# Delta-rule attention and two feed-forward layers on one core: a queue order from step-by-step rules, replaced by a list schedule over a recorded graph

## The chip, the cores and the metric

One core of a Trainium2 chip runs the program. The metric is device time in microseconds (us) of one execution; three runs of the kernel before are shown, and the profile is of one execution. TensorE (PE) multiplies, with weight loads beside it (PEld); VectorE (DVE), ScalarE (ACT) and GpSimd (POOL) do elementwise work; SyncE (SP) issues the DMAs. Each engine takes its own queue strictly in order, so the order in which the program writes instructions is the order in which they wait.

## The reference, cut to what matters

```
# q, k, v: (4, 8, 768, 48)   beta: (4, 8, 768)
k_n = k / (norm(k) + 1e-6)
for t in range(768):                       # per batch and head, state is 48 x 48
    y[t]  = q[t] @ state
    v_old = state^T k_n[t]
    state += beta[t] * outer(k_n[t], v[t] - v_old)
x = y as (3072 tokens, 384)
x = leaky(x @ w1_in) @ w1_out              # leaky(h) = max(0.01 h, h), d_ff 2048
out = (h - tanh(h)) @ w2_out               # h = x @ w2_in
```

The recurrence runs over the sequence; the two feed-forward layers (FFN) need all heads of a token and nothing of later tokens. The kernel works in pairs of 16-bit numbers (a high and a low part of each value, three products for each matrix product).

## The kernel before

**Work.** The sequence is cut into 12 blocks of 64 positions, n = 0 to 11; two of them make a unit, u = 0 to 5. The attention of a block is done in chunked form: `keys` normalizes and splits the keys, `grams` transposes them (matmuls with `ident2`) and forms the products of keys with keys (matmuls `KTp`, `KTp`) into the tile `Gd`; `inverses` (once per unit) solves a triangular system of 32 columns, row by row, into the tile `X`: 30 steps of two small elementwise instructions, `Gd<-X` and `X<-X,Gd`, each on what the one before left; `merges` (matmuls `X`, `AT` and then `XF`, `PM`) puts the halves together; `states`, `products` and `outputs` carry the state on and give the block's tokens, 256 of them over four batches. `to_xa` scales and splits them into a room `x`. That is the first FFN's input.

**FFN.** `layer(n, i)` does block n through layer i, in the order of units: first layer for both blocks of the unit, then second layer for both. A layer has 8 parts; a part is `h_part` (18 matmuls of 256 columns, then the activation, then a split into `g`, whose low half is a subtraction of two tiles in SBUF) and, three parts later, `o_part` (18 matmuls of 256 columns, or in the second layer 12 of 384). `to_xb` scales the first layer's result for the second.

**Weights.** The four weight matrices arrive as 64-bit floats. `w_f32` turns a chunk into 32-bit floats with three passes on DVE; `convert` adds up squares on ACT; then a scale is known and `splits` makes the 16-bit halves (one pass on ACT, one on DVE, one DMA). The raw chunks wait in parts of other weight tiles (`wo`, `wi1`), in two `x` rooms and in the tile `stage`.

**What sets the order.** Everything is issued while Python runs, by rules that look at modelled clocks (`Plan`, with its `cost` and `issue`). The FFN loop is in front: `h_part` calls `Side.step` after every second or third matmul, and `Side` lets a waiting attention or weight generator go on where its inputs are ready by the model and where `idle` says that ACT and DVE are not too far ahead of PE. Thirty numbers each in `START` and `STEADY` (delays per generator, leads, biases) shape it. Elementwise work with two possible engines is placed when it comes up: `tt` takes POOL or DVE for the low half of `g`, the key splits and the masks of `P`; `cp` takes ACT or DVE for copies. The inverse of unit 0 runs on DVE, the others on POOL (`rows` in the tables). Tiles that turn over (`x` 4 rooms, `sx` 4, `g` 4) come from pools by tag. All instructions carry line 160, the one line of `Plan.issue`.

Of the kernel before, what the change touches and what calls it, by code (L numbers as in the profile page):

```python
# [1 line left out]

# [15 lines left out]
KS = 64.0  # L18
POW2 = 0x7F800000
START = {'cp': 1.0, 'lag': 4.0, 'look_pool': 5, 'look_inv': 0, 'lead_k': 1, 'lead_p': 8.2, 'd_v': 1, 'd_xa': 0, 'd_xb': 1, 'k_m': 1, 'd_s0': 4.0, 'd_s1': 2.5, 'd_s2': -1, 'd_s3': 2.7, 'bias_i': 3.5, 'bias': 1.5, 'rep': 3, 'every': 3, 'd_k0': 3, 'd_o': 0.5, 'd_s': 0.0, 'd_p': 1.5, 'd_m': 0, 'd_i': 3, 'd_g0': -2, 'd_q': 4.4, 'd_g': 0.2, 'd_k': 1, 'd_w': 1.5, 'rows': 2}  # L20
STEADY = {'cp': 5.5, 'lag': 3.7, 'look_pool': 5, 'look_inv': 2.5, 'lead_k': 1, 'lead_p': 6.8, 'd_v': 1, 'd_xa': -1.3, 'd_xb': 1, 'k_m': 1, 'd_s0': 1.0, 'd_s1': -0.5, 'd_s2': -1, 'd_s3': 0.5, 'bias_i': 3, 'bias': 4, 'rep': 6, 'every': 2, 'd_k0': 3, 'd_o': 0.5, 'd_s': 0.0, 'd_p': 0, 'd_m': 1.5, 'd_i': 0, 'd_g0': -0.7, 'd_q': 3.4, 'd_g': 0.7, 'd_k': 0, 'd_w': 0, 'rows': 32}


class Plan:
# [3 lines left out]

    GAP = 0.15
    TICK, WARM = 10.24 / 3, 3060  # L30

    def __init__(self, nc):
        self.t = dict(pe=0.0, act=0.0, dve=0.0, pool=0.0, sp=0.0)
        self.dma = 0.0
        self.columns = {}
        self.mem = {}
        self.ring = {}
        self.filler = None
        self.eng = dict(pe=nc.tensor, act=nc.scalar, dve=nc.vector, pool=nc.gpsimd, sp=nc.sync)

    def tile(self, pool, shape, dtype, tag, name, bufs):
        t = pool.tile(shape, dtype, tag=tag, name=name, bufs=bufs)
        old = self.ring.setdefault((id(pool), tag), [])
        free = self.last(old[-bufs]) if len(old) >= bufs else 0.0
        old.append(t.tensor.name)
        self.mem[t.tensor.name] = [(0, 128, 0, 1 << 30, free, True, "")]
        return t

    def free(self, pool, tag, bufs):
        old = self.ring.get((id(pool), tag), [])  # L50
        return self.last(old[-bufs]) if len(old) >= bufs else 0.0

    def last(self, name):
        return max([e[4] for e in self.mem[name]], default=0.0)

    @staticmethod
    def region(ap):
        step, n = ap.ap[0]
        size = SIZE[ap.dtype]
        lo = ap.offset % step  # L60
        hi = lo + 1 + sum(s * (c - 1) for s, c in ap.ap[1:])
        return ap.offset // step, ap.offset // step + n, lo * size, hi * size

    def after(self, ap, write, eng=""):
        es = self.mem.get(ap.tensor.name)
        if not es:
            return 0.0
        p0, p1, lo, hi = self.region(ap)
        psum = ap.space == bass.MemoryType.PSUM
        t = 0.0  # L70
        for q0, q1, l, h, te, w, e in es:
            if (w or write or psum) and not (eng == "pe" and e == "pe"):
                if psum or (p0 < q1 and q0 < p1 and lo < h and l < hi):
                    t = max(t, te + self.GAP)
        return t

    def at(self, *aps):
        return max(self.after(a, False) for a in aps)

    def note(self, ap, t, write, eng):  # L80
        p0, p1, lo, hi = self.region(ap)
        es = self.mem.setdefault(ap.tensor.name, [])
        es[:] = [e for e in es if not ((write or not e[5] and e[6] == eng) and p0 <= e[0] and e[1] <= p1
                                       and lo <= e[2] and e[3] <= hi)]
        es.append((p0, p1, lo, hi, t, write, eng))

    def warm(self, t):

        return self.columns.get(int(t / self.TICK) - 1, 0) >= self.WARM

    def cost(self, eng, op, aps, accum=False):
        n = 1
        for a in aps:
            m = 1
            for d in a.shape[1:]:
                m *= d
            n = max(n, m)
        if eng == "pe":
            n = 1
            for d in aps[-1].shape[1:]:  # L100
                n *= d
            rows = 0.52 if aps[1].shape[0] <= 64 else 1.0
            return rows * n / (2400.0 if self.warm(self.t["pe"]) else 1200.0) + 0.001
        if eng == "act":
            return 0.1 + n * 0.0008 + (0.15 if accum else 0.0)
        if eng == "pool":
            return 0.1 + n * (0.0009 if op == "memset" else 0.002)
        fast = all(SIZE[a.dtype] == 2 for a in aps)
        sbuf = all(a.space != bass.MemoryType.PSUM for a in aps)
        r = 960.0  # L110
        if op == "memset":
            r = 1920.0
        elif op == "transpose":
            r = 480.0
        elif op in ("tensor_copy", "tensor_scalar") and sbuf:
            r = 3840.0 if fast and op == "tensor_copy" else 1920.0
        return 0.065 + n / r

    def ready(self, eng, reads, writes):
        t = 0.0  # L120
        for a in reads:
            t = max(t, self.after(a, False, eng))
        for a in writes:
            t = max(t, self.after(a, True, eng))
        return t

    def finish(self, eng, op, reads, writes):
        return max(self.t[eng], self.ready(eng, reads, writes)) + self.cost(eng, op, writes + reads)

    def issue(self, eng, op, args, kw):  # L130
        writes = [kw[n] for n in ("out", "accum_out") if n in kw]
        rest = list(args)
        if "out" not in kw:
            writes.append(rest.pop(0))
        isap = lambda a: hasattr(a, "tensor")
        reads = [a for a in rest + [v for n, v in kw.items() if n not in ("out", "accum_out")] if isap(a)]
        if eng == "sp":
            s = self.t["sp"]
            for a in writes:
                s = max(s, self.after(a, True))  # L140
            for a in reads:
                s = max(s, self.after(a, False))
            self.t["sp"] = s + 0.05
            self.dma = max(self.dma, s) + kw["out"].free_nbytes() * 128 / 300e3
            t = self.dma + 2.0
        else:
            if self.filler and eng == "dve":
                self.filler(self.ready(eng, reads, writes))
            s = self.t[eng] = max(self.t[eng], self.ready(eng, reads, writes))
            t = self.t[eng] = s + self.cost(eng, op, writes + reads, "accum_out" in kw)  # L150
            if eng == "pe":
                n = int(t / self.TICK)
                self.columns[n] = self.columns.get(n, 0) + writes[0].free_nbytes() // 4 * reads[0].shape[0] // 128
        for a in writes:
            if a.tensor.name in self.mem or a.space != bass.MemoryType.DRAM:
                self.note(a, t, True, eng)
        for a in reads:
            if a.space != bass.MemoryType.DRAM:
                self.note(a, t, False, eng)
        return getattr(self.eng[eng], op)(*args, **kw)  # L160


class Part:


    def __init__(self, aps, banks):
        self.aps, self.banks = aps, banks


class Engine:  # L170
    def __init__(self, plan, name):
        self.plan, self.name = plan, name

    def __getattr__(self, op):
        return lambda *args, **kw: self.plan.issue(self.name, op, args, kw)


class Room:


    def __init__(self, plan, pool, bufs):
        self.plan, self.pool, self.bufs = plan, pool, bufs

    def tile(self, shape, dtype, name, tag=None, bufs=None):
        return self.plan.tile(self.pool, shape, dtype, tag or name, name, bufs or self.bufs)

    def free(self, tag, bufs=None):
        return self.plan.free(self.pool, tag, bufs or self.bufs)


@with_exitstack
def kernel(
    ctx: ExitStack,
    tc: tile.TileContext,
    q: bass.AP,
    k: bass.AP,
    v: bass.AP,
    beta: bass.AP,
# [3 lines left out]
    w2_out: bass.AP,  # L202
    out: bass.AP,
):
    plan = Plan(tc.nc)
    pe, act, dve, pool, sp = (Engine(plan, n) for n in ("pe", "act", "dve", "pool", "sp"))
    NU, D = k.shape[0], k.shape[4]
    NM = k.shape[3]
# [133 lines left out]
    def at(*aps):  # L342
        return plan.at(*aps)
# [894 lines left out]
```

## Time and profile before

| what | us |
|---|---|
| three runs: lowest, median, highest | 1198.43, 1198.58, 1199.84 |
| span of the profiled execution, first to last instruction | 1199.5 |
| PE busy | 1005.0 (84%), 16216 matmuls |
| DVE busy | 738.1 (62%) |
| ACT busy | 592.5 (49%) |
| POOL busy | 419.2 (35%) |
| chain that ended last, by engine | PE 48%, DVE 25%, POOL 12%, ACT 8% |
| mean granted clock of TensorE | 0.974 of full |

The profiled execution's own time is not listed apart from its span; the span lies 0.9 us over the median of the three runs and inside their spread. An engine's busy share is a mean over stages that differ: the first eighth of the span prepares weights and the first block, the middle mixes attention with FFN, and the last quarter is nearly FFN alone. A group's line shows busy time, the mean length of one instruction in ns, and the idle time before it with what ended it.

### The profile page before, as it was taken

What the parts mean: (1) busy time and instruction counts of PE and PEld (TensorE: products, weight loads), DVE (VectorE), ACT (ScalarE), POOL (GpSimd) and SP (SyncE); (2) the same over time, 40 slices, a digit from 0 to 9 for tenths busy, and PEclk for the clock granted to TensorE, in tenths of its full rate; (3) what the DMA queues carried; (4) which work ended last, traced back from release to release, by engine and by line L of the source; (5) the groups of instructions that cost most, each with busy time, mean ns of one, the idle gap of its engine ahead of it and who ended that gap; (6) DMA issues with size and microseconds to landing.
All of it is one profiled execution on the core that took longest, in us unless ns stands there. A gap on an engine that the chain in (4) does not pass through costs nothing.

```text
span 1199.5 us, 36733 instructions
## 1 busy us (share of the span) xinstructions
PE 1005.0 (84%) x16216; PEld 823.4 (69%) x16216; DVE 738.1 (62%) x1600; ACT 592.5 (49%) x1311; POOL 419.2 (35%) x520
## 2 busy tenths in 40 slices
PE   0200887499798998987999989999999999999998
PEld 0200866387476886765788867788877888778875
DVE  7998789877567665678658666456673154420242
ACT  3533566755355764464555734535543354333332
POOL 4201033259312793168414861386110230012100
PEclk9999999799898999989999999999999999999999
DMA  9440325311101200011100100001000000000001
GB/s 361 156 134 23 109 70 181 118 61 34 28 21 29 60 1 16 3 47 27 35 25 25 32 15 17 15 2 34 25 11 14 15 11 2 14 14 1 1 1 27
DMA packets 30559, 54.45 MB, mean 45 GB/s; under 512 B 4800, under 2 KB 16064, under 8 KB 30400
## 3 DMA queue, kind: packets, MB, share of 16 engines
q1 hardware_dynamic: 30400, 52.11, 13.8%
q8 instruction: 126, 2.06, 0.7%
q14 instruction: 33, 0.27, 0.1%
HBM read 41.09 MB, written 4.72 MB: 38 GB/s over the span
## 4 chain that ended last, share of the span: by engine, by line
PE 48%; DVE 25%; POOL 12%; ACT 8%; issue 5%; DMA 2%; SPq 0%; POOLq 0%; DVEq 0%; ACTq 0%
PE o L160 19%; PE h_ps L160 18%; PE a_ps L160 11%; POOL X L160 6%; POOL Gd L160 4%; DVE wi L160 4%; DVE wo L160 2%; DVE x L160 2%; DVE X L160 2%; DVE g L160 2%; ACT g L160 2%; DVE Gd L160 2%; DVE sx L160 1%; DVE Ub L160 1%; DVE Sb L160 1%
## 5 line engine op out<-in xcount | busy, mean ns | idle before, releaser
L160 PE MATMUL h_ps<-x,wi 128*128 128x256 f16 x3456 | 433.6, 279 | 24.7 <-DVE sx L160 13.3
L160 PEld LDWEIGHTS <-wi 128*128 128x128 f16 x3456 | 338.9, 100 | 91.0 <-issue 35.4
L160 PE MATMUL o<-wo,g 128*128 128x384 f16 x1152 | 210.8, 331 | 7.3 <-ACT osb L160 4.8
L160 PE MATMUL o<-g,wo 128*128 128x256 f16 x1728 | 210.4, 274 | 1.3 <-DVE osb L160 1.3
L160 POOL TENSOR_TENSOR g<-sx,g 128x512 f16<-128x512 f32 x74 | 88.9, 1201 | 320.1 <-ACT g L160 313.7
L160 PEld LDWEIGHTS <-wo 128*128 128x128 f16 x1728 | 166.4, 98 | 25.1 <-issue 3.7
L160 ACT ACTIVATE g<-sx 128x512 f16<-128x512 f32 x192 | 121.0, 630 | 122.1 <-DVE sx L160 119.0
L160 PEld LDWEIGHTS <-g 128*128 128x128 f16 x1152 | 111.9, 99 | 74.6 <-issue 13.6
L160 DVE SCALAR_TENSOR_TENSOR sx<-sx,kap,h_ps 128x512 f32<-128x512 f32 x96 | 71.0, 740 | 96.9 <-ACT sx L160 96.4
L160 DVE SCALAR_TENSOR_TENSOR g<-sx,g 128x512 f16<-128x512 f32 x96 | 76.6, 798 | 67.1 <-ACT g L160 67.1
L160 ACT ACTIVATE sx<-h_ps 128x512 f32<-128x512 f32 x96 | 56.6, 590 | 102.9 <-PE h_ps L160 100.2
L160 ACT ACTIVATE sx<-h_ps,kap 128x512 f32<-128x512 f32 x96 | 65.4, 682 | 81.1 <-PE h_ps L160 72.3
L160 POOL TENSOR_TENSOR X<-X,Gd 128x30 f32<-128x30 f32 (+9 forms) x150 | 97.2, 648 | 11.8
L160 PEld LDWEIGHTS <-KTp 64*64 64x64 f16 x3360 | 63.4, 115 | 53.0 <-issue 49.7
L160 POOL TENSOR_TENSOR P<-P,maskp 128x1024 f16<-128x1024 f16 x24 | 56.3, 2348 | 120.9 <-DVE P L160 115.7
L160 POOL TENSOR_TENSOR Gd<-X 128x30 f32<-128x30 f32 (+9 forms) x150 | 89.0, 593 | 26.4 <-DVE X L160 14.9
L160 PE MATMUL a_ps<-ab,ones 128*128 128x1 bf16 x124 | 11.3, 166 | 101.1 <-DVE ab L160 100.6
L160 PEld LDWEIGHTS <-KN 64*64 64x64 f16 x1824 | 37.2, 119 | 38.5 <-issue 30.7
L160 DVE COPY Ub<-R 64x768 f16<-64x768 f16 x46 | 24.4, 530 | 39.7 <-PE a_ps L160 39.2
L160 POOL MEMSET XF<- 32x512 f32 x12 | 6.2, 519 | 112.9 <-PE a_ps L160 109.9
L160 PEld LDWEIGHTS <-ones 128*128 128x128 bf16 x124 | 7.8, 100 | 52.5 <-issue 38.3
L160 PE MATMUL a_ps<-Q,Sb 128*128 128x64 f16 x528 | 32.8, 194 | 10.8 <-DVE Sb L160 10.8
(163 smaller groups left out, 1451.2 us busy)
## 6 DMA issues: line engine op xcount, KB each, us to landing
wo<-in_w_in_dram SPq DMA_DIRECT2D x32, 384.0 KB, 6.2
qf<-in_q_dram SPq DMA_DIRECT2D x24, 256.0 KB, 3.0
wi<-in_w_out_dram SPq DMA_DIRECT2D x14, 384.0 KB, 7.8
kf<-in_k_dram SPq DMA_DIRECT2D x12, 384.0 KB, 3.4
vf<-in_v_dram SPq DMA_DIRECT2D x12, 384.0 KB, 3.2
out_dram<-osb SPq DMA_DIRECT2D x48, 96.0 KB, 2.2
wi<-wh SPq DMA_DIRECT2D x16, 192.0 KB, 2.7
wo<-wh SPq DMA_DIRECT2D x16, 192.0 KB, 2.5
```

The lines of the kernel that those rows point to most:

```text
L160: return getattr(self.eng[eng], op)(*args, **kw)
```

## The change

The kernel body now records instead of issuing. `Graph.put` and `Graph.matmul` make nodes (a run of matmuls into one bank is one node), `depend` draws the edges from overlapping reads and writes, `tails` computes for each node the longest path to the end, and `schedule` walks through time: of the nodes that are ready on an engine it takes the one with the longest path. `issue` then writes out that order. `START`, `STEADY`, `Plan`, `Side` and all generators go. Where two engines are allowed for a node (`either`), the schedule picks one when the node comes up.

```diff
+    def tails(self, share=1.2, stretch=1.0, extra=1.0):
+        for n in reversed(self.nodes):
+            t = tail[n.idx]
+            for m in n.succs:
+                t = max(t, tail[m.idx] + self.LAT[m.main])
...
+            a, b = heap[e]
+            if b and lock <= t + 1e-9 and (not a or b[0] < a[0]):
+                p, i, alt = heappop(b)
+            elif a:
+                p, i, alt = heappop(a)
...
-    NA, NX, NSX = 4, 4, 4
...
+    x_r = ring("x", 6, KT * N, order=False)
+    x_r.most["a"] = 5
+    s_r = ring("sx", 4, 512, short=True)
+    g_r = ring("g", LAG + 1, 512)
...
-    stage = wts.tile([128, 2 * DM * 2], F32, name="stage")
...
+    def inv_eng(u):
+        return "dve" if u == 0 else "pool"
...
+    def p_engs(n):
+        return ("dve",) if n < 4 else ("pool",)
...
+    def k_engs(n):
+        return ("dve",)
...
         if i == 0:
             copy(g[:, 0], sx)
-            tt(g[:, 1], sx, g[:, 0], ALU.subtract, bias())
+            tt(g[:, 1], sx, g[:, 0], ALU.subtract, TWO)
...
-        side.step(max(at(x[0], WI[i][:, 2 * p]), ps_h.free("h")))
...
+    for u in range(NU):
+        for s in range(2):
+            if u:
+                if s == 0:
+                    load_b(u, 0)
+                    load_b(u, 1)
+                keys(2 * u + s)
+            grams(2 * u + s)
+        nat = inverses(u)
+        merges(u, nat)
+        for s in range(2):
+            n = 2 * u + s
+            queries(n)
+            products(n)
...
+    g_.prepare()
+    order, _ = g_.schedule(g_.tails())
     with tc.manual_schedule():
...
+        g_.issue(order)
```

Rooms are now tiles of their own (`x0` to `x5`, `g0` to `g3`, `sx0` to `sx3`, `gd0`, `xi0`) that are written again and again instead of pool tiles; `stage` is gone, and its 6 KB per partition are the two more `x` rooms. The masks of `P` run on DVE for blocks 0 to 3 and on POOL afterwards; the key splits run on DVE alone. The matmuls are the same in number: 1728 of each first product, 1728 and 1152 of the second products, 9880 small ones. On the other queues DVE's subtractions for `g` go from 22 to 93 and POOL's from 74 to 3; copies of `Ub` and `Sb` on DVE go from 89 to 39 and on ACT from 3 to 53; POOL's masks of `P` go from 24 to 16.

**PE, from the first FFN matmul.** `h_ps` (now `ps_h0`) is the first FFN product, `ident2` with `KN` the transposition of a block's keys; `KN2` (room 2 of 4) holds those of block 2. Before, two places of the queue:

```order
L160 MATMUL a_ps_2087<-ab_1985,ones_101 128x1
L160 LDWEIGHTS wi0_104
L160 MATMUL h_ps_2139<-x_169,wi0_104 128x256
...
L160 LDWEIGHTS KN2_112
L160 MATMUL a_ps_2171<-ident2_97,KN2_112 64x64
```

Now:

```order
L413 MATMUL ps_a0_88<-ab1_93,ones_127 128x1
L413 LDWEIGHTS KN2_137
L413 MATMUL ps_a0_88<-ident2_123,KN2_137 64x64
...
L413 MATMUL ps_a0_88<-pq0_81,KTp1_140 64x64
L413 LDWEIGHTS wi0_131
L413 MATMUL ps_h0_84<-x0_61,wi0_131 128x256
```

The transposition of block 2 stood behind the first FFN matmuls and now stands ahead of them, and so do all 192 key products of unit 1.

**POOL, around the inverse of unit 1.** `gd0` was `Gd`, `xi0` was `X`; `tri` and `bt` (`b10`) are the factors of the Gram tile; rows `128x30` begin the solve. Before:

```order
L160 TENSOR_TENSOR g_3597<-sx_3595,g_3597 128x512
L160 TENSOR_TENSOR Gd_2138<-Gd_2138,tri_103 128x256
L160 TENSOR_TENSOR Gd_2138<-Gd_2138,bt_657 128x256
...
L160 TENSOR_TENSOR g_3831<-sx_3829,g_3831 128x512
L160 TENSOR_TENSOR Gd_2138<-X_3892 128x30
L160 TENSOR_TENSOR X_3892<-X_3892,Gd_2138 128x30
```

Now:

```order
L416 TENSOR_TENSOR gd0_79<-gd0_79,tri_129 128x256 x4
L416 TENSOR_TENSOR gd0_79<-gd0_79,b10_110 128x256 x4
L416 MEMSET wacc0_111 128x16
L416 TENSOR_SCALAR b00_109<-b00_109 128x32
L416 TENSOR_TENSOR gd0_79<-gd0_79,tri_129 128x256
...
L416 TENSOR_TENSOR gd0_79<-xi0_80 128x30
L416 TENSOR_TENSOR xi0_80<-xi0_80,gd0_79 128x30
```

Behind unit 0's Gram tiles the solve of unit 1 had 13 subtractions for `g` and 6 masks of `P` in front of it; it is now the first thing that POOL does behind the Gram tiles of units 0 and 1.

**DVE, around the split of the first block's tokens.** `COPY x` is the last step before the first FFN matmul can go; `wi1`, `wo0` rows are weight passes. Before:

```order
L160 SCALAR_TENSOR_TENSOR x_169<-x_169,sxs_1872,xhi_2105 128x768
L160 COPY x_169<-xhi_2105 128x768
L160 SCALAR_TENSOR_TENSOR wi1_105<-wo1_107,wi1_105 128x768
L160 CAST ab_2113<-sc_1882 128x1
L160 TENSOR_SCALAR wi1_105<-wo1_107 128x768
```

Now:

```order
L416 SCALAR_TENSOR_TENSOR x0_61<-x0_61,sxs0_113,sx3_70 128x768
L416 TENSOR_SCALAR wi1_132<-wo1_134 128x768
L416 COPY x0_61<-sx3_70 128x768
...
L416 TENSOR_TENSOR pq1_82<-pq1_82,maskp_124 128x1024
L416 SCALAR_TENSOR_TENSOR wo0_133<-wo0_133,sw_130,sx2_69 128x2x384
L416 TENSOR_TENSOR g0_71<-sx1_68,g0_71 128x512
```

The `COPY x` was DVE's 291st instruction and is now its 324th; a mask of `P` and the low half of `g`, which were POOL's there, stand in DVE's queue behind it.

## Rows read from the trace of the kernel before

**Rows 1.** The page: PE's busy tenths in 40 slices of 30 us.

```profile
PE   0200887499798998987999989999999999999998
```

**Rows 2.** Windows: length, busy us of PE, PEld, DVE, ACT, POOL; granted clock; DMA.

```profile
0.00:156.00 156.00, 43.41 (x1366) 40.33 (x1367) 132.96 (x291) 62.49 (x141) 28.83 (x40) 1.00 0.43 151
156.00:414.00 258.00, 217.02 (x3713) 175.65 (x3713) 193.76 (x394) 157.82 (x372) 110.23 (x129) 0.93 0.23 70
414.00:923.00 509.00, 473.85 (x8497) 386.36 (x8496) 323.65 (x721) 264.75 (x621) 239.06 (x318) 0.98 0.07 20
1062.00:1194.00 132.00, 132.00 (x1098) 106.99 (x1095) 32.35 (x68) 47.28 (x77) 18.48 (x16) 1.00 0.03 7
```

**Rows 3.** Timeline of PE: where three first-layer passes begin.

```profile
156.01 2.08 PE L160 MATMUL h_ps<-x,wi 128*128 128x256 f16 x9 [4.80 <-DVE x L160]
223.41 3.69 PE L160 MATMUL h_ps<-x,wi 128*128 128x256 f16 x18 [1.13 <-DVE x L160]
413.58 1.80 PE L160 MATMUL h_ps<-x,wi 128*128 128x256 f16 x15
```

**Rows 4.** Chain that ended last, 250 to 330 us: start, length, piece.

```profile
252.85 1.63 PE a_ps L160 x96
...
261.42 1.52 POOL Gd L160
...
307.98 2.36 POOL X L160
...
322.31 2.40 PE a_ps L160 x144
```

**Rows 5.** Chain at full clock (two pieces), and timeline of PE around 48 wide matmuls.

```profile
1052.42 1.95 PE o L160 x12
1054.37 1.96 PE h_ps L160 x18
...
193.23 0.25 PE L160 MATMUL a_ps<-Q,Sb 128*128 128x64 f16 x3
...
194.62 2.13 PE L160 MATMUL o<-g,wo 128*128 128x256 f16 x18
```

**Rows 6.** Groups of DVE by form: busy us, mean ns, idle before.

```profile
L160 DVE TENSOR_TENSOR g<-sx,g 128x512 f16<-128x512 f32 x22 | 24.8, 1126 | 24.7 <-ACT g L160 21.6 <-POOL Gd L160 3.1
L160 DVE SCALAR_TENSOR_TENSOR n<-n 128x16 f32<-128x16 f32 x60 | 14.1, 235 | 2.1
L160 DVE SCALAR_TENSOR_TENSOR Gd<-a_ps,maskb,Gd 128x256 f32<-128x256 f32 x24 | 11.5, 479 | 6.1 <-ACT Gd L160 5.8
L160 DVE SCALAR_TENSOR_TENSOR wi<-wo,wi 128x768 int32<-128x768 int32 x32 | 34.8, 1089 | 0.6
L160 DVE TENSOR_TENSOR Gd<-X,Gd 128x1024 f16<-128x1024 f32 x6 | 8.1, 1356 | 15.0 <-ACT Gd L160 15.0
```

**Rows 7.** Timeline of DVE in the first 30 us: start, length, instruction.

```profile
8.16 2.17 DVE L160 TENSOR_SCALAR PM<-ident 128x512 f16<-128x512 f16 x1 [6.63 <-POOL PM L160]
...
26.03 1.27 DVE L160 TENSOR_TENSOR KN<-kn,KN 128x384 f16<-128x384 f32 x1
...
28.56 0.54 DVE L160 TENSOR_TENSOR KN<-kn,KN 128x384 f16<-128x384 f32 x1
```

**Rows 8.** Waits of PE from 414 to 924 us: total, times, longest.

```profile
PE a_ps L160 <- DVE Sb L160: 7.9, 7, 2.4
PE h_ps L160 <- DVE sx L160: 6.6, 2, 3.4
PE a_ps L160 <- DVE ab L160: 5.7, 5, 2.2
PE a_ps L160 <- issue: 3.5, 5, 1.3
PE o L160 <- ACT osb L160: 3.0, 3, 1.4
```

**Rows 9.** The same from 156 to 414 us, the largest.

```profile
PE a_ps L160 <- DVE ab L160: 19.0, 6, 9.3
```

More of the change, by code (lines that the diff above doesn't have):

```diff
@@ L117, in cost @@
[L117 to L145, printed above, removed]
-        else:
[L147 to L160, printed above, removed]
@@ L163 @@
[L163 to L188, printed above, removed]
+            d = 0.12 + n * {"memset": 0.0008, "tensor_scalar": 0.001}.get(op, 0.00205)
@@ new lines, in ffn, with prepare @@
+    def ffn(self, node):
+        node.chain, self.last_ffn, node.ffn = self.last_ffn, node, True
+    def prepare(self):
+        for n in self.nodes:
+            n.preds.discard(n)
+            n.first = set(n.preds)
+            for b in n.new:
+                if b.ring.short:
+                    n.first |= {m for u in b.users for m in u.preds if m.idx < n.idx}
+            n.first |= {b.users[0] for b in n.bufs if b.users[0] is not n}
+            n.late = n.first - n.preds
+            for m in n.preds:
+                m.succs.append(n)
+            for m in n.late:
+                m.after.append(n)
+            if "pe" in n.calls:
+                n.cost = {"pe": (n.warm + 0.17, n.warm, False)}
+                n.dma = 0
+            n.main = next(iter(n.calls))
@@ new lines, in tails @@
+    def tails(self, share=1.2, stretch=1.0, extra=1.0):
+        tail = [0.0] * len(self.nodes)
+        for n in reversed(self.nodes):
+            t = tail[n.idx]
+            for m in n.succs:
+                t = max(t, tail[m.idx] + self.LAT[m.main])
+            d = n.cost[n.main][0] + (2.3 + n.dma / self.RATE if n.dma else 0.0)
+            if not n.ffn:
+                d = d * stretch + extra
+            tail[n.idx] = t + d
+            if n.chain is not None:
+                tail[n.chain.idx] = max(tail[n.chain.idx], t + n.warm * share)
+        return [-t for t in tail]
@@ L237, with fixed, ring @@
-    ps_a = room("ps_a", NA, space=bass.MemoryType.PSUM)
-    done = set()
-    def tune(name):
-        return (STEADY if "w2" in done else START)[name]
+    sbuf = ctx.enter_context(tc.tile_pool(name="sbuf", bufs=1))
+    psum = ctx.enter_context(tc.tile_pool(name="psum", bufs=1, space=bass.MemoryType.PSUM))
+    def fixed(name, shape, dtype):
+        t = sbuf.tile(shape, dtype, tag=name, name=name)
+        return View(t[tuple(slice(0, s) for s in shape)], Buf())
+    def ring(name, rooms, width, pool=sbuf, short=False, order=True):
+        ts = [pool.tile([128, width], F32, tag=f"{name}{i}", name=f"{name}{i}") for i in range(rooms)]
+        return Ring(name, [t[:, 0:width] for t in ts], short, order)
@@ L358, in words @@
         n = DM * 2
-        return [t[:, i * n:(i + 1) * n] for i in range(t.shape[1] // n)]
+        return [(t, i * n) for i in range(t.shape[1] // n)]
     def w_f32(parts):
@@ L829, in states @@
         if not zero:
-            yield from wait(("f", n - 1))
             for g in range(NG):
@@ L1094 @@
-    side = Side()
-    xa_t, xb_t = {}, {}
-    def all_outputs():
-        for n in range(NS):
-            yield from outputs(n)
+        ts(kap[:, 2:3], sw[:, 3:4], C0, None, ALU.mult)
+        recip(kap[:, 3:4], kap[:, 2:3])
+        tt(kap[:, 2:3], kap[:, 3:4], kap[:, 0:1], ALU.mult)
     pend = []
-    def need(key):
-        while key not in done:
-            side.force()
     def o_next():
@@ new lines @@
+    for n in range(2):
+        load_k(n)
+    for i in range(2):
+        load_b(0, i)
+    load_v(0, 0)
+    consts()
+    for t in (Ub, Sb, PM):
+        memset(["pool"], t, 0.0)
+    memset(["pool"], AT[:, :, 0], 0.0)
+    ts(PM[:, 0, :, HB:], ident2[:, HB:].unsqueeze(1).to_broadcast([128, NM, HB]), -KS, None, ALU.mult)
+    for t in KN:
+        memset(["pool"], t[:, :, :, :, D:].rearrange("p g c m d -> p (g c m) d"), 0.0)
+    first_keys()
+    xw = [words(g_.tile(x_r, [128, 2 * DM], F32))[0] for _ in range(2)]
@@ L1195, in lay_out @@
+    for u in range(NU):
+        for i in range(2):
+            for s in range(2):
+                layer(2 * u + s, i)
+    while pend:
+        o_next()
+    g_.prepare()
+    order, _ = g_.schedule(g_.tails())
+    with tc.manual_schedule():
+        g_.issue(order)
 def lay_out(q, k, v, beta, moe_w_in, moe_w_out, moe2_w_in, moe2_w_out):
```

1220 lines of the change are left out of this document (591 added, 629 removed).

## The prediction

> **What bounds the kernel now.** I read the busy slices first, to see where PE is idle. In [rows 1] the first four slices, 120 us, are almost empty; from the sixth on PE shows mostly 8 and 9. So there are two kinds of loss, the time before the first FFN matmul and the gaps later, and the windows [rows 2] give their sizes. Up to 156.0 us DVE is busy for 133.0 us and PE for 43.4: DVE's queue is the bound there (its 291 instructions end in the `COPY x` that the first FFN matmul waits for, [rows 3]). From 156 to 414 us PE is idle for 41 us and runs at a granted clock of 0.93, so a seventh of its matmul time passes with the lower of its two levels (1.2 and 2.4 GHz). From 414 to 923 it is idle for 35.2 us at 0.98. In the last window PE is busy for 132.00 of 132 us: nothing is to be had there.
>
> A floor comes next. Parts cost 1.95 to 1.96 us at full clock, 48 wide matmuls 1.39 (from 193.23 to 194.62) [rows 5], 144 small ones 2.40, or 16.7 ns each [rows 4]. Over both queues' 384 FFN parts, 1104 wide and about 8900 small matmuls that is about 938 us; 24 of them lie ahead of the first FFN matmul. From that matmul (156.01 us) to PE's end (1194) the kernel takes 1038 us for 914 of work: **124 us are lost behind the start**. From the fourth first-layer pass (413.58, [rows 3]) it takes 780 us for 227 + 80 parts, 768 wide, 5280 small matmuls, 715 us: 65 lost there, 59 between.
>
> What loses them is read from the chain and the waits. Between 250 and 330 us the chain is unit 1's inverse: its last key product at 252.85, POOL's solve from 261.42 to 310.3, the first matmul that uses it at 322.31 [rows 4]: 69 us, 49 of them on POOL. In the old order PE has only 54 to 70 us of work between these two places of a unit (61 in the middle), by the queue's counts. Later the waits are small and spread: 26.7 us in five kinds [rows 8].
>
> **The change part by part.** *The start.* By the queues, 324 DVE instructions stand up to the first `COPY x`, 33 more. Eight weight passes fewer: 8 x 1.089 = -8.7. Gram low halves, 8 x 0.479 = +3.8; the scalar passes of the key norm, 15 x 0.235 = +3.5 [rows 6]. Eleven key subtractions move in from POOL, at 0.54 to 1.27 us [rows 7]; I take 0.7, the nearer to the one without POOL beside it, as POOL is idle for most of this stage: +7.7. Three masks of `P`: no row shows them on DVE. At least 0.54 as the key subtraction with 384 elements, at most 1.36 x 1.5 = 2.0 by the 1024-element subtraction of 32-bit numbers [rows 6] with room above it; I take 1.3: +4. The rest (three low halves, a transposition of 1024 elements, eight scalars, eight copies fewer) I put at +1.6, between -2 and +6. Sum +12, between +4 and +20. In return the queue no longer begins with 6.63 us of waiting for POOL's memset of `PM` [rows 7]; keys come up first and I take 4 of it, between 0 and 6.6. First FFN matmul: 156 + 12 - 4 = **164 us**.
>
> *From the first FFN pass to the fourth.* This was 257.6 us. The second pass waits for the second `COPY x`. Between the two copies DVE's queue held 62.3 us by its durations and took 67.4 us, a factor 1.08; now it holds 39.6, so 42.8 us, while PE's work there is 27: second pass at 207. Behind it the second layer needs the weights: 35.6 x 1.08 = 38 us of DVE against 32 of PE: 245. Then PE's own work: 33 (unit 1's grams and transpositions no longer lie here), 53 and 38 us. Fourth first-layer pass at 245 + 33 + 53 + 38 = **369 us**, 44.6 earlier. DVE could reach that copy at about 362, so it is not the bound.
>
> *The inverse.* All key products of unit 1 now stand ahead of the first FFN matmul, and in the units behind it the queue has 102 us of PE work or more (127 for unit 1) between a unit's last key product and the first use of its inverse. The solve is at the head of POOL's queue. Its 69 us fit with 33 to spare, so I cost the chain at nothing; the cover is FFN work and costs, if gone, what is over 102.
>
> *The moves between engines.* 71 more subtractions for `g` on DVE at 1.126 are 80 us over twelve blocks, and 50 copies go to ACT. DVE's queue sums to 118 us for a unit in the middle, where PE needs about 157: hidden, and POOL is freed. A `g` has three parts, 5.9 us, until its second product, and the subtraction takes 1.126 [rows 6]. I cost it at nothing. By the Trainium skill's "SBUF — State Buffer", section "Who interferes with whom", a DVE instruction with both inputs in SBUF and a GpSimd instruction that reads SBUF block each other, the later one wholly. The trace agrees in kind: 1.27 us beside POOL against 0.54 without. By that rule the moved subtractions could hold up POOL's solve; this is a rival below.
>
> *Rooms.* Two more for `x` let a block's tokens be ready earlier; they remove waits and add none. The raw chunks lose the stage tile, and the fetch of weights has 0.43 of DMA's share in the start [rows 2], so I cost it at nothing; if chunks came late, DVE's start would move by that.
>
> *The rest.* From the fourth pass PE has 227 parts x 1.96 + 80 x 1.95 + 768 x 0.029 + 5568 x 0.0167 = 716 us, with norm products and the banks' first matmuls 720. Of the 65 us that were lost here I keep 20: below the 26.7 us of [rows 8] as the longest-path order puts the carried state earlier, above half of them (13), since each of these waits is a short handover that no order removes wholly. 369 + 720 + 20 = 1109; behind PE's end the output takes 5.5 us (1199.5 - 1194): 1114.5. The span stands 0.9 over the median of the runs, so **1114 us**, bounds 1090 to 1140.
>
> **The rivals.**
> *Late losses stay.* The 65 us behind the fourth pass are not the inverse's but handovers on DVE and ACT, which the change leaves alike: 369 + 720 + 65 + 5.5 - 0.9 = 1159. For it: none of the waits of [rows 8] names the solve. Against: they sum to 26.7, and a lower clock (0.98) follows idle time. Chance 0.20.
> *Nearly no losses.* The start costs nothing more (156) and PE never waits behind 369: 1085 to 1094. For it, the last window. Chance 0.15.
> *A new wait in PE's queue: slower.* PE's order is fixed from modelled durations. 51 norm groups of PE (49 before) stand between FFN matmuls, each on a DVE `ab` cast. If DVE's longer queue brings these late, the whole FFN waits behind each. The six such waits of [rows 9] took 3.2 us each; 51 of them are 162: 1094 + 162 = 1256. It decides from 105 / 51 = 2.05 us each. Against: in 414 to 924 us only five waits, 1.1 us each, were of this kind [rows 8]. Chance 0.09.
> *POOL's solve blocked by DVE.* If each POOL step waited for a DVE subtraction as long as itself, 49 us become 98, the chain 118 against 102 of cover: 16 x 5 units = 80 us, 1194, no gain. It decides from 82 us on POOL. Against: at most 16 such subtractions fall into a 98 us stretch, 16 x 1.126 = 18 us: 67 on POOL. The page named above has the rule; the factor is mine. Chance 0.04.
> *The change doesn't do what it says.* If the modelled durations are so far off that the order idles as the old one did: about 1199. Against: the old order rests on the same kind of model, and the room that it gives the inverse is counted in PE work, not in modelled time. Chance 0.04.
>
> **How the numbers follow.** The forecast has 0.48. A measurement of this kernel can tell some 0.2% (2.4 us) from no change. Faster: 0.48 + 0.20 + 0.15 and part of the last two, 0.86; slower 0.11; same 0.03. The range goes from 1080, below the case without losses and its start's lower bound, to 1165, above the case where late losses stay: 0.83 of the chance.
>
> **What would show it.** Right: the first FFN matmul at 160 to 172 us, the second pass at about 207, the fourth near 369; no solve on the chain between 250 and 330 us; PE idle for about 20 us behind the fourth pass. The forecast is wrong if PE's largest waits are for DVE's `ab`, if a product of `X` with `AT` waits long for DVE or ACT, or if DVE is over nine tenths busy in the middle.

## The result, and the profile after

| | before | changed |
|---|---|---|
| median of the runs, us | 1199.21 | 1101.15 (1100.77 to 1106.44) |
| ratio | 1 | 0.9171, 95% interval 0.9136 to 0.9206 |
| span of the profiled execution, us | 1199.5 | 1098.8 |

The forecast was 1114 us in 1080 to 1165. The time is 13 us below it. The 100.7 us between the two spans lie in three places: 11.8 ahead of the first FFN matmul, 48.7 from there to the fourth first-layer pass, 40 from there to PE's end.

The changed kernel's page, PE's busy tenths and its granted clock in 40 slices of 27.5 us:

```profile
PE   2215689989899999999999999999999999999998
PEclk9655689999999999999999999999999999999999
```

The gaps that [rows 1] shows at the start are shorter, and from the twelfth slice on PE is full. The granted clock reads 0.5 or 0.6, at or near its lower level, from the second slice to the fifth, in which PE is busy for one to six tenths; the first slice reads 0.9. The page of the kernel before reads 0.9 in its first four slices, though PE is almost idle there, so the two pages can't be compared in this row for the start, nor by their mean clocks (0.974 and 0.952).

Windows of the changed kernel (columns as in [rows 2]), cut at 144 us, where its first FFN matmul starts:

```profile
0.00:144.00 144.00, 52.95 (x1827) 49.54 (x1829) 122.97 (x324) 92.00 (x268) 37.71 (x64) 0.66 0.48 168
144.00:414.00 270.00, 252.22 (x3629) 210.90 (x3622) 213.88 (x468) 180.35 (x394) 88.91 (x117) 0.99 0.21 62
414.00:923.00 509.00, 502.23 (x8740) 416.05 (x8739) 305.35 (x693) 297.06 (x603) 172.53 (x235) 1.00 0.08 22
923.00:1062.00 139.00, 139.00 (x1809) 115.70 (x1807) 58.33 (x138) 67.75 (x116) 5.79 (x4) 1.00 0.04 9
```

PE's idle time from the first FFN matmul to 414 us was 41 us [rows 2] and is 17.8; from 414 to 923 it was 35.2 and is 6.8, and the granted clock there went from 0.98 to 1.00. Ahead of the first FFN matmul PE now does 1827 matmuls in place of 1366.

Timeline of PE in the changed kernel: the first, second and fourth first-layer pass, and PE's last piece (a pass begins with its first `h_part`):

```profile
144.17 8.04 PE L413 MATMUL ps_h<-x,wi 128*128 128x256 f16 x72
...
179.53 2.13 PE L413 MATMUL ps_h<-x,wi 128*128 128x256 f16 x18
...
353.05 2.13 PE L413 MATMUL ps_h<-x,wi 128*128 128x256 f16 x18
...
1085.58 7.96 PE L413 MATMUL ps_o<-wo,g 128*128 128x384 f16 x48
```

They answer to 156.01, 223.41 and 413.58 [rows 3]. What PE waits for from 414 us to its end is nearly nothing. Of the five kinds of [rows 8] four have gone, the norm groups (`ab`) among them, and `issue` is as large as before (3.5 us):

```profile
PE ps_a L413 <- issue: 3.6, 5, 1.1
PE ps_a L413 <- DVE R L416: 2.8, 4, 1.0
PE ps_a L413 <- DVE x L416: 0.2, 1, 0.2
```

### The profile page after: what moved, and what is told of

Read it like the earlier page. It is cut to its first block, busy times and chain, and to the rows that moved or that the text cites. A ratio compares the mean times of both kernels' runs of the same rounds, so it can differ in the third digit from the quotient of the medians.

```text
span 1098.8 us, 36802 instructions
## 1 busy us (share of the span) xinstructions
PE 977.9 (89%) x16216; PEld 814.5 (74%) x16216; DVE 711.8 (65%) x1636; ACT 647.4 (59%) x1396; POOL 304.9 (28%) x419
## 4 chain that ended last, share of the span: by engine, by line
PE 71%; DVE 16%; ACT 5%; DMA 5%; issue 3%; SPq 0%; ACTq 0%
PE ps_o L413 29%; PE ps_h L413 29%; PE ps_a L413 13%; DVE wi L416 4%; DVE wo L416 2%; DMA wo<-in_w_in_dram 1%; ACT jk L416 1%; DVE g L416 1%; DVE R L416 1%; DMA x<-in_w_out_dram 1%; DVE pq L416 1%; ACT sx L416 1%; DVE n L416 1%; DVE sx L416 1%; DVE xi L416 1%
## 5 line engine op out<-in xcount | busy, mean ns | idle before, releaser
L413 PE MATMUL ps_h<-x,wi 128*128 128x256 f16 x3456 | 413.7, 273 | 3.9 <-DVE sx L416 2.6
L413 PE MATMUL ps_o<-g,wo 128*128 128x256 f16 x1728 | 206.1, 273 | 5.2 <-DVE g L416 3.5
L413 PE MATMUL ps_o<-wo,g 128*128 128x384 f16 x1152 | 208.6, 326 | 1.0 <-DVE x L416 1.0
L416 DVE TENSOR_TENSOR g<-sx,g 128x512 f16<-128x512 f32 x93 | 70.1, 753 | 110.4 <-ACT g L416 110.3
L416 ACT ACTIVATE sx<-ps_h 128x512 f32<-128x512 f32 x96 | 56.9, 594 | 132.8 <-PE ps_h L413 123.0
L416 DVE SCALAR_TENSOR_TENSOR sx<-sx,kap,ps_h 128x512 f32<-128x512 f32 x96 | 71.5, 745 | 86.7 <-ACT sx L416 86.5
L416 ACT ACTIVATE sx<-ps_h,kap 128x512 f32<-128x512 f32 x96 | 65.5, 682 | 93.5 <-PE ps_h L413 81.8
L416 POOL TENSOR_TENSOR xi<-xi,gd 128x30 f32<-128x30 f32 (+9 forms) x150 | 102.0, 680 | 11.4
L416 POOL TENSOR_TENSOR gd<-xi 128x30 f32<-128x30 f32 (+9 forms) x150 | 95.1, 634 | 27.2 <-DVE xi L416 10.8
L416 ACT ACTIVATE jk<-kf 128x48 bf16<-128x48 f32 x160 | 38.2, 239 | 3.8 <-DMA kf<-in_k_dram 0.8
```

The costliest lines, as they stand in the source:

```text
L413: self.eng["pe"].matmul(out=o.real(), lhsT=lhsT.real(), rhs=rhs.real(), start=start, stop=stop)
L416: getattr(self.eng[n.on], op)(**{k: v.real() if isinstance(v, View) else v for k, v in kw.items()})
```

## The experiments

All are the changed kernel with one edit or a few, but for one, which is the kernel before. Ratios are against the kernel before, run beside it (medians 1202.1 to 1203.9 us); differences in us are against the changed kernel's 1101.15.

**1. Four rooms for x.**

```diff
-    x_r = ring("x", 6, KT * N, order=False)
-    x_r.most["a"] = 5
+    x_r = ring("x", 4, KT * N, order=False)
+    x_r.most["a"] = 3
```

> The changed kernel with four rooms for x in place of six (at most three for tokens in place of five). Theory A (the order does it, the rooms are idle): in the changed order every x is x0 to x3, so nothing moves, 1098 to 1105 us. Theory B (the two more rooms are what lets blocks be ready early): tokens wait for a room again, 1115 us or more, with waits of ACT or DVE for a room of x ahead of the FFN passes.

Measured: 1100.81 us, ratio 0.9148 (0.9126 to 0.917). The order written out names `x0` to `x3` alone in either kernel; the fifth and sixth room are never taken. This part of the change is worth nothing, and the run shows how close two executions of one order lie.

**2. All first-layer low halves of `g` on POOL.**

```diff
-            tt(g[:, 1], sx, g[:, 0], ALU.subtract, TWO)
+            tt(g[:, 1], sx, g[:, 0], ALU.subtract, ("pool",))
```

> The changed kernel with all 96 low halves of g in the first layer on POOL, as 74 of them were before. Theory A (order): POOL's busy time grows by 93 x 1.2 = 112 us to about 417, DVE's falls by 70; the order is made anew around it, the unit's solve takes longer but has 100 us of cover: 1101 to 1120 us. Theory C (the placement does it: POOL freed for the solve): the solve is late again and PE waits for it, more than half of the 98 us gained goes, 1150 us or more.

Measured: 1111.36 us, ratio 0.9237 (0.9217 to 0.9257), 10 us of the 98 gone. POOL is busy for 396.6 us (304.9 in the changed kernel). The first FFN matmul stays at 144.8; the loss lies before 414 us, where PE is busy for 244.73 of 270 us in place of 252.22. From 414 to 923 it is as full as with `g` on DVE (503.79). Theory A holds.

**3. Three parts undone: four rooms, `g` and all masks of `P` on POOL.**

```diff
-        return ("dve",) if n < 4 else ("pool",)
+        return ("pool",)
```

(with the edits of 1 and 2)

> The changed kernel with three parts undone together: four rooms for x, all low halves of g in the first layer on POOL, all masks of P on POOL. What is left of the change is the list order. Theory A: at least two thirds of the gain stay, 1101 to 1132 us. Theories B or C: 1150 us or more.

Measured: 1118.2 us, ratio 0.9295 (0.9271 to 0.9319): 83% of the gain stays with these old places (1202.6 - 1118.2 = 84 of 101 us). Two other moves stay in this kernel and were not undone in any run: the key splits are on DVE alone, and the copies of `Ub` and `Sb` are still shared out between DVE and ACT by the schedule. Its windows, from 144 us:

```profile
144.00:414.00 270.00, 232.99 (x3372) 196.19 (x3371) 191.45 (x399) 170.65 (x377) 133.22 (x160) 0.94 0.21 64
414.00:923.00 509.00, 502.83 (x8627) 416.87 (x8625) 275.46 (x651) 297.38 (x600) 208.29 (x280) 1.00 0.08 21
```

Again the whole loss is in the stretch in which POOL works most (133 us); the middle is full at 502.83. PE's largest wait there is for ACT. Here ACT's queue has weight passes in front of the FFN activation (from 187.95 to 206.82 us), not POOL's solve:

```profile
PE ps_h L413 <- ACT sx L416: 20.2, 6, 16.4
```

**4. The same walk, but the node recorded first goes first.**

```diff
-    order, _ = g_.schedule(g_.tails())
+    order, _ = g_.schedule([n.idx for n in g_.nodes])
```

> The changed kernel with the same walk through time, but among ready nodes it takes the one recorded first, not the one with the longest path. Theory A (longest paths matter): attention of later units and weight passes go ahead of what the next FFN pass needs, the first FFN matmul is later by tens of us: 1140 to 1210 us. Theory D (any order that lets PE take whatever is ready fills the gaps as well): at most 1115 us.

Measured: 1191.44 us, ratio 0.9906 (0.9882 to 0.993). Rooms, placements and the walk are all there, and 90 of the 98 us are gone. Its first two windows, and PE's largest wait over the whole run:

```profile
0.00:144.00 144.00, 17.85 (x566) 16.47 (x567) 132.34 (x303) 82.29 (x206) 16.03 (x33) 0.60 0.70 234
144.00:414.00 270.00, 228.38 (x5291) 200.36 (x5290) 212.25 (x531) 179.81 (x467) 111.09 (x160) 0.82 0.11 32
```

```profile
PE ps_a L413 <- DVE ab L416: 73.7, 14, 28.7
```

DVE spends the start on weight passes, 566 matmuls are done by 144 us, and the first FFN matmul comes at 212.67. The wait for `ab` (a norm of something whose inputs were put last) is the largest one of the kernel before too (100.6 us in 16 waits); in both, most of it lies ahead of the first FFN matmul. So a walk that fills idle engines isn't enough; the longest path has to say with what.

**5. The key products held back.** The matmuls of a unit's second block of keys (units 1 to 5) wait in the order for the FFN matmul that stood 55 us ahead of the first use of the inverse:

```diff
+    ffn, late = [n for n in g_.nodes if n.ffn], []
+    for u in range(1, NU):
+        use = next(n for n in g_.nodes[marks[u, 3]:] if "pe" in n.calls)
+        f = max((n for n in ffn if g_.start[n.idx] <= g_.start[use.idx] - 55.0), key=lambda n: g_.start[n.idx])
+        late += [(f, n) for n in g_.nodes[marks[u, 1]:marks[u, 2]] if "pe" in n.calls and f not in n.first]
+    for f, n in late:
+        n.first.add(f)
+        f.after.append(n)
+    order, _ = g_.schedule(g_.tails())
```

(`marks` are places in the list of nodes.)

> The changed kernel, with the key products of each unit's second block (units 1 to 5) held back in the order until the FFN matmul that stood 55 us ahead of the first use of the unit's inverse; the order is then made anew. So the cover of the inverse goes from 102 us or more of PE work to about 55, as before the change. Theory A (the cover is what took the inverse off the path): the inverse's 69 us are short of cover by 14 us or more per unit, PE waits for X (or the FFN runs dry behind it): 1112 to 1170 us. Rival (the inverse was never what cost the time): 1098 to 1106 us.

Measured: 1109.41 us, ratio 0.9203 (0.917 to 0.9235). Neither theory's number: 8 us more than the changed kernel. Unit 1's solve starts on POOL at 219.58 in place of 118.16, and the third first-layer pass moves from 312 to 331 us, but the fourth only from 353 to 360, and from 414 on little is lost (PE 502.45 of 509). So the shorter cover costs something mostly in unit 1. In a list order, which is made anew around it, the inverse's cover is worth at most these 8 us, not the larger part of the gain; what it cost under the old rules, which could not move other work into the gap, this run doesn't say.

**6. The walk without its port rule.** The walk lets no instruction of POOL overlap, in its own time, with a DVE instruction that has two inputs in SBUF or is a fast copy. The kernel before had no such term in `Plan.cost` or `Plan.issue`.

```diff
-            if locked:
-                lock = t + dur - (0.05 if e == "dve" else 0.0)
```

> The changed kernel, with the one rule of its walk removed that keeps DVE instructions with two inputs in SBUF (or fast copies) and POOL instructions from overlapping in modelled time. Theory P (the start came earlier than the sum of old durations because the order keeps the two engines apart): DVE's weight passes and subtractions get longer again (the subtraction for g from 753 ns towards 1126), the first FFN matmul comes at 150 us or later, 1106 to 1130 us. Rival (the durations fell by themselves): first FFN matmul at 142 to 147 us, 1098 to 1106 us.

Measured: 1165.67 us, ratio 0.967 (0.964 to 0.97), 64 us worse, far more than either theory said, and not by longer DVE instructions: the subtraction for `g` takes 757 ns (753 with the rule), the weight pass 946 (964). The first FFN matmul comes at 167.6 us, as theory P had it (150 or later), but the theory falls in its mechanism. The chain of waits has 20% of its span on POOL, which the changed kernel's chain doesn't name among its engines at all. By the second first-layer pass 47 us are lost (226.9 for 179.5).

**7. The kernel before with `g` on DVE.**

```diff
-            tt(g[:, 1], sx, g[:, 0], ALU.subtract, bias())
+            tt(g[:, 1], sx, g[:, 0], ALU.subtract, -1000.0)
```

> The kernel before, with one part of the change alone: all low halves of g in the first layer on DVE (before: 22 on DVE, 74 on POOL); its rules make the rest anew. Theory C (placement is the gain): POOL's solve starts 10 us or more earlier and the time falls to 1150 us or less. Theory A (order): 1180 to 1215 us.

Measured: 1206.51 us, ratio 1.0021 (0.9999 to 1.0042). In the old rules the placement gives nothing: theory A's range holds, and theory C's 1150 us don't come. But the run is no clean test of it: the rules, made anew, also put unit 1's solve on DVE (from 261.4 to 300.6 us, the start of the solve as before), which is much of why POOL is busy for only 42.24 us from 144 to 414 us (111.54 before), and POOL's solves of the later units start later, not earlier (unit 2 at 419.3 for 405.6). So POOL's freed time was never used for an earlier solve here; experiments 2 and 3 are the test of the placement.

**8 and 9. Jitter, with the rule.** Is 64 us perhaps what any small disturbance of such an order does?

```diff
+    import random
+    random.seed(16)
+    order, _ = g_.schedule([p * (1 + 0.002 * (random.random() - 0.5)) for p in g_.tails()])
```

> The changed kernel with every node's priority multiplied by a random number between 0.999 and 1.001, so that near ties fall otherwise: what the order is worth by chance alone. Theory A (the longest paths as such): 1095 to 1110 us. Rival L (this one order is a lucky draw and neighbours of it are much worse, so the 64 us of the run without the port rule are such a draw): 1120 us or more.

> The same with another seed. Theory A: 1095 to 1110 us; rival L: 1120 us or more.

Measured: 1098.35 us, ratio 0.9144 (0.9106 to 0.9182), and, with seed 10, 1104.79, ratio 0.9189 (0.9159 to 0.9219). Both orders drawn anew land within about 4 us of the changed kernel's; the faster of the two isn't told apart from it, as the intervals overlap. So the 10 and 8 us of experiments 2 and 5 are little over these two draws; the 17 of 3 and the 90 of 4 lie well over them. Single stages move more than the whole: the first FFN matmul comes at 134.7 and 140.8 us (144.2 in the changed kernel), the fourth pass at 351.7 and 358.6 (353).

**10 and 11. Jitter, without the rule.** The edits of 6 and 8, with seeds 4 and 17.

> No port rule in the walk, and jittered priorities with a seed for which the walk's own clock ends no later than that of the changed kernel, so the order isn't a bad one by its own lights. Theory M (without the rule the walk believes in overlaps of DVE and POOL that the chip doesn't give, and PE's fixed queue then waits for late ones): 1125 us or more, with single waits of PE over 10 us behind the first FFN matmul. Theory L (the earlier run without the rule was an unlucky order): 1095 to 1115 us.

> The same with another seed of that kind. Theory M: 1125 us or more; theory L: 1095 to 1115 us.

Measured: 1136.49 us, ratio 0.9453 (0.9422 to 0.9485), and 1144.53, ratio 0.9519 (0.9487 to 0.955). Some 39 us worse than 8 and 9 in the mean (1140.5 against 1101.6), so about 25 of the 64 us of experiment 6 were its draw, and 39 are the rule, by two draws on each side. Of the 39, the larger part lies behind the fourth pass: from there to PE's end the two take 771 and 761 us, where 8 and 9 take 739. Theory M holds in size. Of PE's single waits over 10 us there is one, in the eleventh kernel (10.63 us, for POOL's `XF` at 159.97); the tenth has 6.5 at most. But its seven waits for ACT's `sx` sum to 29.4 us (22.2 in the eleventh; 7.4 and 5.4 in 8 and 9). ACT's queue in the tenth kernel, around the end of the solve of unit 3, shows how:

```profile
529.24 0.60 ACT L414 ACTIVATE sx<-ps_h 128x512 f32<-128x512 f32 x1 [2.67 <-PE ps_h L411]
529.87 0.63 ACT L414 ACTIVATE g<-sx 128x512 f16<-128x512 f32 x1
537.66 1.33 ACT L414 ACTIVATE gd<-xi 128x1024 f16<-128x1024 f32 x1 [7.16 <-POOL xi L414]
538.86 0.57 ACT L414 ACTIVATE sx<-ps_h 128x512 f32<-128x512 f32 x1
```

and PE's queue at the same time:

```profile
532.97 2.13 PE L411 MATMUL ps_o<-g,wo 128*128 128x256 f16 x18
539.48 3.49 PE L411 MATMUL ps_h<-x,wi 128*128 128x256 f16 x18 [4.38 <-ACT sx L414]
```

The copy of the solved `xi` stands at the head of ACT's queue for 7.16 us before POOL is done. Behind it stands the activation of the next FFN part; until that has read its bank, PE has no bank for the part after, and waits 4.38 us. The part behind the gap took 3.49 us, too, in place of 2.13; the granted clock is 0.60 from 539.4 to 543.0 us and 1.00 before the gap (520 to 533). Over the run ACT waits in this way five times:

```profile
ACT gd L414 <- POOL xi L414: 35.2, 5, 9.3
```

In the changed kernel this wait doesn't appear at all. The solves themselves take no longer on POOL (42.8 to 50.8 us for units 2 to 5 with the rule, 43.7 to 45.4 without it): it is not the solve that got longer, it is the copy that is queued too early. The walk's own times show it: for units 3 to 5 it takes the 60 steps of a solve for 36 to 37 us in the tenth kernel, where the chip takes 45, and for 46 to 49 in the changed kernel, where the chip takes 47 to 51.

**12. Without the rule, but POOL's modelled times 1.4 times as long.**

```diff
-            d = 0.12 + n * {"memset": 0.0008, "tensor_scalar": 0.001}.get(op, 0.00205)
+            d = 1.4 * (0.12 + n * {"memset": 0.0008, "tensor_scalar": 0.001}.get(op, 0.00205))
```

(with the edits of 6 and 8, seed 11)

> As in the two jittered kernels without the port rule, but the walk takes every POOL instruction for 1.4 times as long: a step of the solve then costs in the walk about what it takes on the chip beside DVE, with no word of ports. In those two, ACT waited 35.2 and 27.3 us at the head of its queue for POOL's solve, with the FFN's activations behind it. Theory M2 (what the port rule gives is only a solve of the right length, so that ACT's copy of it is queued late enough): ACT's wait for the solve falls under 10 us, PE idles under 12 us from 414 to 923, 1100 to 1118 us. Rival N (it is the overlaps themselves, on all instructions): 1128 us or more, as without the rule.

Measured: 1115.18 us, ratio 0.9284 (0.9254 to 0.9315). ACT's wait for the solve is gone, and the window that answers to the third one above reads

```profile
414.00:923.00 509.00, 496.12 (x8654) 411.41 (x8653) 306.68 (x697) 299.42 (x601) 165.82 (x229) 1.00 0.07 21
```

so PE idles for 12.9 us there (M2 said under 12), 23.6 in the tenth kernel, 6.8 in the changed one. The walk takes the solves of units 3 to 5 for 49 to 51 us here, the chip 47. M2 is right for about 25 of the 39 us, in one order: with POOL's durations right in the walk they don't arise. The edit lengthens all of POOL's work, so the run doesn't part the solve from the rest of it. Some 14 us are left. About 4 are there by the fourth pass (358.0 us, against 353.1, 351.7 and 358.6 with the rule), the rest behind it (747.3 us to PE's end, against 739 to 740.5), and which overlap costs them stays open.

**What the walk foresaw.** `schedule` returns, beside the order, the time at which its own clock ends. It is a model's number, but it tells a bad order from a wrong model:

| order | walk's end, us | measured, us | difference |
|---|---|---|---|
| changed kernel | 1049.7 | 1101.15 | 51 |
| 8 and 9, jitter | 1047.5, 1053.8 | 1098.35, 1104.79 | 51, 51 |
| 2, 3 and 5 | 1063.0, 1073.7, 1059.5 | 1111.36, 1118.2, 1109.41 | 48, 45, 50 |
| 4, recorded order | 1125.0 | 1191.44 | 66 |
| 6, 10 and 11, no port rule | 1068.5, 1047.4, 1051.3 | 1165.67, 1136.49, 1144.53 | 97, 89, 93 |
| 12, no rule, long POOL | 1051.2 | 1115.18 | 64 |

With the rule the chip is 45 to 51 us behind the walk in all six orders by longest paths, and without it 89 to 97. So 19 of the 64 us of experiment 6 were in its order by the walk's own clock, and what the rule keeps away is about 38 to 46 us in each of the three draws; POOL's longer times alone keep away some 25 to 33 of them. The losses of experiments 2 and 5 were foreseen, too (13 and 10 us for 10 and 8 measured), which speaks for their being more than chance.

## Why the prediction was right, and where it was off

**The start: the term was mis-sized by 20 us, and its sign was wrong.** The prediction added 12 us of DVE work, took off 4, and had the first FFN matmul at 164; it came at 144.17. The count was right, 33 DVE instructions more up to the first `COPY x`. The sum was not. Grouped by form, the recorded durations of these instructions add up to 142.7 us before and 148.3 now, so 5 to 6 more, not 12: weight passes and splits -10.8, all work on the keys +3.3 (the splits alone were taken as +7.7), Gram low halves +3.8 as said, norm +2.4, masks +2.3 (taken as 4), transposition and low halves of `P` and queries +4.3. But DVE's busy time in the stretch fell from 133.0 [rows 2] to 122.97 us, ten less. The durations overlap, by 9.7 us before and by 25.3 now, and the sum of means counts that time twice. The 4 us for DVE's idle time at the start were nearer: it idled for 23 us before and for 21 now.

Why they overlap more is seen in the solve of unit 0, whose 60 steps each need the one before. Timeline of DVE in the kernel before:

```profile
69.46 0.40 DVE L160 TENSOR_TENSOR Gd<-X 128x228 f32<-128x228 f32 x1
69.89 0.40 DVE L160 TENSOR_TENSOR X<-X,Gd 128x228 f32<-128x228 f32 x1
70.21 0.95 DVE L160 SCALAR_TENSOR_TENSOR wo<-wi,wo 128x768 int32<-128x768 int32 x1
```

and in the changed kernel:

```profile
63.56 0.39 DVE L416 TENSOR_TENSOR gd<-xi 128x228 f32<-128x228 f32 x1
63.87 0.95 DVE L416 SCALAR_TENSOR_TENSOR wi<-wo,wi 128x768 int32<-128x768 int32 x1
64.74 0.39 DVE L416 TENSOR_TENSOR xi<-xi,gd 128x228 f32<-128x228 f32 x1
```

A step that needs the one before starts 0.43 us after it; an instruction that doesn't, 0.31 us after a step of the same size. The old rules issued the solve in runs of six steps, so 50 of its 59 pairs of steps followed directly; the list order puts a weight pass or a norm step between all of them, since the next step isn't ready and the other is. At about 0.12 us for each of 50 pairs that is some 6 us, an estimate from these rows. It is only a part: in the whole stretch 124 DVE instructions began before the recorded end of the one in front, and 281 do now, so two thirds of the added overlaps lie outside the solve. No run tried this by itself; and the draws of 8 and 9 alone move the first FFN matmul to 134.7 and 140.8 us.

**From the first to the fourth pass: right in size, by errors that cancel.** Forecast 205 us (164 to 369), measured 208.9. In its parts: 35.4 us to the second pass for 43, 33.7 for 38, then 38.6, 60.3 and 41 for 33, 53 and 38: 12 too much, then 16 too little. That the sum fits is luck in part. In the first two parts the weights' DVE work was again dearer in the sum than on the chip: PE was to stand idle for 22 us in them (43 against 27 of work, 38 against 32), and in all five it idles for 17.8. What makes the later three longer was not tried.

**The inverse: right that it goes off the path, wrong in what that is worth.** POOL's solve is on no chain piece from 250 to 330 us. But it doesn't take the 49 us of POOL that the prediction carried over: unit 1's takes 113 (118.16 to 231.3), as two subtractions for `g` stand between its steps, at the head of POOL's queue and waiting for ACT:

```profile
160.82 2.46 POOL L416 TENSOR_TENSOR g<-sx,g 128x512 f16<-128x512 f32 x1 [21.07 <-ACT g L416]
199.18 1.16 POOL L416 TENSOR_TENSOR g<-sx,g 128x512 f16<-128x512 f32 x1 [29.66 <-ACT g L416]
```

That costs nothing only because the cover is long: ACT takes up the solved tile at 270 us. Experiment 5 took the cover away and lost 8 us. The prediction didn't price the step; it let the reader think that the inverse was what lost the time between passes. In the list order it is worth the smaller part; how much of those passes it cost under the old rules was not tried.

**The moves between engines: costed at nothing, and worth about 10.** 71 more subtractions on DVE were to be hidden. They are; on POOL they cost 10 us (experiment 2), 17 with the masks (3), the first of which is little over the draws of 8 and 9. Each takes 753 ns now, not the 1126 of [rows 6]:

```profile
L416 DVE TENSOR_TENSOR g<-sx,g 128x512 f16<-128x512 f32 x93 | 70.1, 753 | 110.4 <-ACT g L416 110.3
```

**The rooms: wrong.** They were said to let tokens be ready earlier. In the changed kernel's order they are never used.

**Late losses: the sum was right, its halves weren't.** From the fourth pass to PE's end 740 us were forecast (720 of work, 20 lost), and 740.5 measured (353.05 to 1093.54). PE idles there for about 7 us, so 13 of the 20 are work that was priced too low. (The terms as listed add up to 711 us where the prediction's floor has 715, and to 932 where it has 938; only the later sum names what was added.) That no order removes these handovers wholly was wrong: 26.7 us in [rows 8] became 6.6. The kernel before lost 36 of its 65 us there by idling, and the rest is put down to the clock and to the same low price: PE was busy for 744.98 us from the fourth pass on and is for 733.72 now, with 292 more matmuls. The last term, 0.9 us off for the runs' time against the span, had the wrong sign: the profiled execution of the changed kernel took 1101.25 us for a span of 1098.8. The order alone closes this stage: it is as full with the old places (502.83 us busy of 509, experiment 3) as with the new.

**The rivals.** *Late losses stay* (1159) fell with the waits above. *Nearly no losses* (1085 to 1094) came closest in the late stage, seven us of idle time, and the measured 1101 lies nearer to its range than to the forecast's 1114. *A new wait in PE's queue* named the wrong producer, the norm groups: these cost 0.7 us behind the first FFN matmul. But its mechanism, a queue fixed from durations that the chip doesn't keep, is what experiments 6, 10 and 11 show, on ACT and with POOL's solve as the late one; by these runs the port rule keeps it away here. *POOL's solve blocked by DVE* put 67 us on POOL with the moved subtractions; the solves of units 2 to 5 took 43 to 51. *The change doesn't do what it says* was argued away with "the old order rests on the same kind of model". That was wrong: the old rules' clocks have no term for POOL beside DVE, and the new ones without it lose 39 us. Whether such a term would have helped the old rules was not tried. Of the prediction's own signs of being right only the solve off the chain came as said: the passes came 16 to 28 us early, and PE idled for 7 us in place of 20 behind the fourth.

The Trainium skill's "SBUF — State Buffer", section "Who interferes with whom", has the port pair that DVE and GpSimd share as an exclusive lock, for which a DVE instruction with two inputs in SBUF and a GpSimd instruction that reads SBUF contend. The trace agrees in kind. Timeline of the changed kernel, a DVE instruction of that sort and two steps of one form on POOL, one beside it and one behind it:

```profile
331.47 1.08 DVE L416 TENSOR_TENSOR g<-sx,g 128x512 f16<-128x512 f32 x1
332.08 0.94 POOL L416 TENSOR_TENSOR gd<-xi 128x240 f32<-128x240 f32 x1
...
333.87 0.62 POOL L416 TENSOR_TENSOR gd<-xi 128x240 f32<-128x240 f32 x1
```

The step that starts beside the subtraction is 0.32 us longer than the other. The prediction used the page to ask whether instructions get longer; what mattered was whether the plan knows that they do.

## What to carry to other kernels

An order fixed ahead of time is as good as its longest paths and its durations: taking ready work in the recorded order gave back 90 of 98 us, and leaving out one shared resource 39, in good part through a consumer that stood too early at the head of ACT's in-order queue, with the late producer two engines away from the PE that waited. A planner's own end beside the measured time tells a bad order from wrong durations: 51 us lie between them in the changed kernel and both of its draws, 89 to 97 without the rule. When such a wait shows up for ACT or DVE, look at what stands in front of the instruction named, not at the instruction. And before a scheduling gain is put down to the resources that came with it (rooms, a move to another engine), run the new order with each of them undone.

## What the runs showed of the hardware that was not expected

The sum of recorded DVE durations is not DVE's time: 148.3 us of them took 122.97. In the solve's rows above an instruction that doesn't need its forerunner starts about 0.08 us before that one's recorded end, one that does need it 0.03 after. So this dependent chain on DVE is cheaper by about a tenth of a microsecond per step when other work is put between its steps. The Trainium skill's "VectorE: DVE Perf Modes", section "The DRAIN you can't avoid", says that the next instruction doesn't start until the pipe is empty, and that one which is not held starts earlier. The rows above have a start 0.03 us behind the recorded end and one 0.08 ahead of it; whether being held is what parts the two, no run shows.

What stands at the head of an engine's queue holds up all behind it: 7.16 us on ACT in the tenth kernel, which cost PE 4.38, and 21.07 and 29.66 on POOL in the changed one, which cost nothing.
